# Seven half-size products for two more experts of the second pass, and the last weights' conversion spread over the expert passes

## The chip, the cores and the metric

One core of a Trainium2 chip runs the whole kernel. The metric is the time on the device in microseconds (us), median of the runs; less is better. The engines are TensorE (PE in the profile, PEld its weight loads), VectorE (DVE), ScalarE (ACT), GpSimd (POOL) and SyncE (SP, which only issues DMAs here).

## What is computed

A chain of three stages on 4 x 576 = 2304 tokens of width 512. First a windowed attention with 8 heads. Then a mixture of 8 experts in which every token goes through every expert, weighted by a matrix P that eight rounds of row and column scaling have made:

```
for e in range(8):
    h = np.maximum(x @ w1[e], 0.0)          # 512 -> 1024
    out += P[:, e:e + 1] * (h @ w2[e])      # 1024 -> 512
```

Last, one feed-forward layer with 2048 hidden units, `g(x @ w_in) @ w_out`, where g is a clipped square. `w_in` and `w_out` arrive as 64-bit floats and have to be made 32-bit on the chip. Every 32-bit value is then split into a high and a low part (fp32r), and every product is three matmuls: high x high, high x low, low x high (`product`, L347 to L351).

## The kernel before

Tokens are worked in three passes of 768 (k = 0, 1, 2). A hidden layer is cut in units of 512 hidden columns: an expert is two units (2e and 2e + 1), the feed-forward layer is units 16 to 19. One accumulator `acc` holds the output of the pass.

**First layer of a unit** (`first_layer`, L353): 768 x 512 by 512 x 512 as seven half-size products (a Strassen form; the order is 1, 5, 6, 2, 7, 3, 4), each in two halves q, so 14 steps m = 0 to 13 of six matmuls of 384 columns. At m = 6 to 11 VectorE adds the product to a kept partial sum (L368).

**Second layer** in one of two ways. A unit run (`"u"` in the list of runs) does it plainly: 72 matmuls of 512 columns in 24 steps (`second_layer`). An expert run (`"e"`) takes both units of an expert together and does their second layer as seven half-size products (`seven_second`, L440): 7 products (n = 0 to 6) x 3 token tiles (t = 0, 1, 2) x 12 matmuls of 256 columns = 252. The input of each product is a sum and difference of quarters of the hidden layer (`Seven`, sums on VectorE at L323, high parts on ScalarE at L109, low parts on VectorE at L110), made one step at a time by the tables `FIRST_WORK` and `SECOND_WORK`. After each (n, t) VectorE adds the result into `acc` (L465), in program order with everything else on VectorE. Two 256-column results share one PSUM bank: `halves` (L443) gives t = 0 and t = 2 the two halves of one bank, t = 1 another.

Pass k = 0 runs units singly, since the experts' weights are prepared then. In pass k = 1 the experts named by `WHOLE` (L430) run as two unit runs, the others as expert runs; in pass k = 2 experts 1 to 7 are all expert runs. Expert 0 has its first unit done during the attention and its second one (`u == 1`) as a unit run in each pass.

**The conversion** of `w_in` and `w_out` (`double_steps`, L206) is a generator; each `pull(double)` in the program text puts the next step into the engines' instruction streams at that place. It runs in passes k = 1 and k = 2, and has 14 empty steps, then 352 steps, 88 for each unit: four pieces of `w_in` with seven VectorE operations each (ops 1, 2, 3 and 5 short, ops 4, 6 and 7 long), 28 steps that split that unit's `w_in` (groups of four: a ScalarE copy; a VectorE subtraction; another and a store; a pause), and four pieces of `w_out` with eight steps (the seven operations, then a step with a ScalarE copy, the VectorE subtraction that waits for it, and two stores). It stops at the end of a piece when `at.hold` is set (from expert 6 of pass k = 1 until the first layer of pass k = 2) and then starts again with a load and eight empty steps. What is left at the last expert of pass k = 2 is put out there at once (`drain(double)`).

Every engine works its instructions off in program order, and all DMAs are on SyncE's one queue, also in program order: nothing is reordered at run time.

Of the kernel before, what the change touches and what calls it, by code (L numbers as in the profile page):

```python
# [27 lines left out]
def tile_attention_moe_ffn(ctx: ExitStack, tc, q, k, v, w_gate, w1, w2, w_in, w_out, out):  # L28
# [130 lines left out]
    def prep_w2(u):  # L159
# [3 lines left out]
        for d, (there, here) in enumerate(w2_halves(u)):  # L163
            if d == 0 or u % 2 or u // 2 in WHOLE:
                nc.sync.dma_start(out=there, in_=here)
# [261 lines left out]
                finish(py[t], k * TPP + t)  # L427
            yield "y"

    WHOLE = (1, 2, 3)  # L430

    FIRST_WORK = {1: "h10 h11", 2: "l10", 3: "l11", 4: "s50", 5: "s51 h50", 6: "h51", 7: "l50", 8: "l51",
                  12: "s60 s61", 13: "s70 s71"}
# [436 lines left out]
    def pull(steps, n=1):  # L870
        for _ in range(n):
            next(steps, None)

    with tc.manual_schedule():
# [214 lines left out]
        for k in range(1, NPASS):  # L1089
            runs += [("u", 1, k)]  # L1090
            for e in range(1, E):
                runs += [("u", 2 * e + i, k) for i in range(2)] if k == 1 and e in WHOLE else [("e", e, k)]
        runs += [("u", u, k) for k in range(NPASS) for u in FFN]
# [4 lines left out]
        def input_of(run):  # L1098
            return run[2], units[units_of(run)[0]][0]
# [12 lines left out]
        for n, run in enumerate(runs):  # L1112
            kind, k = input_of(run)[1], run[2]
# [3 lines left out]
            ends = begins(n + 1)  # L1117
# [12 lines left out]
            if run[0] == "u":  # L1130
                u = run[1]
# [49 lines left out]
                for m, s in enumerate(second_layer(k, finish, LAST if u2 is None else SECOND)):  # L1181
                    if fresh and m == 0:
                        if u == 1:
                            load_raw_w2(u2)
                        ahead = prep_w2(u2)
                    if fresh:
                        pull(nxt)
                    if ends and m > 4 and (m % 2 if kind == "ffn" else m % 3 == 0):
                        pull(build)
                    if m > 2 and m % 2:  # L1190
                        at.sink = ("h", 2)
                        pull(sink)
                    if m > 12 or u > 1 and m % 5:
                        pull(double)
                    if m % 3:
                        pull(sums)
# [16 lines left out]
            for m, i in enumerate(first_layer(2 * e, act_kept(0), late)):  # L1213
                if m % 2:
                    pull(nxt)
                if m < 6 or m > 11:
                    pull(double)
                if e == 1 and m >= len(ORDER) * UQ - TPP:
                    t = m - (len(ORDER) * UQ - TPP)
                    nc.scalar.activation(out=acc[:, t, :], in_=acc[:, t, :], func=AF.Copy,  # L1220
                                         scale=prob[:, k * TPP + t, 0:1])
# [14 lines left out]
            for m, i in enumerate(first_layer(2 * e + 1, act_kept(1), late)):  # L1236
                if m % 2:
                    pull(nxt)
                work(ops, FIRST_WORK.get(m, ""))
                if not ends and m < 2:  # L1240
                    pull(double)
            drain(nxt)
            for n_, t in seven_second(e, k, bufs):
                work(ops, SECOND_WORK.get((n_, t), ""))
                if t == TPH - 1:
                    later = n_ + 3
                    if later < len(ORDER):
                        load_op(e, ORDER[later], words(w2_buf[(ring + later) % 3]))
                    elif after[0] == "e":
                        load_op(after[1], ORDER[later - 7], words(w2_buf[(ring + later) % 3]))  # L1250
                if not ends and (n_, t) >= (4, 0):
                    pull(double)
                if ends and (n_, t) in ((1, 2), (2, 2), (3, 2), (4, 1), (4, 2), (5, 0), (5, 1), (5, 2), (6, 0), (6, 1)):
                    pull(build)
# [34 lines left out]
```

## Time and profile before

| | |
|---|---|
| median of 3 runs | 2012.32 us (2011.96 to 2013.23) |
| profiled execution | 2011.22 us, its span 2009.4 us |
| TensorE matmul busy | 1976.8 us, 98% of the span |
| VectorE busy | 1423.2 us, 71% |
| ScalarE busy | 916.4 us, 46% |
| DMA, 16 engines' share | 70.6% |

The span is the time from the first to the last instruction of the profiled execution; the time of that execution is 1.8 us longer, and the median of the runs another 1.1 us. Busy shares are averages over stages with different limits, so the argument goes by stretches: what an expert takes from its first matmul to the next one's, and which wait on TensorE ends when.

### The profile page before, as it was taken

To read this page: it belongs to the slowest core of one execution; us is meant where nothing else is said; L and a number is where in the kernel's file an instruction comes from. 1 tells how busy PE (TensorE), PEld (TensorE's weight loads), DVE (VectorE), ACT (ScalarE), POOL (GpSimd) and SP (SyncE) were. 2 spreads that over 40 slices of the span, in tenths; PEclk is the share of its full clock that TensorE was granted. 3 is DMA by queue.
4 is the path that set the end of the run, shared out by engine and by line. 5 is a ranking of instruction groups with operands and counts; after the bars stand their busy time and mean duration, and the time that the engine had idled before them with its cause. 6 is when DMAs were issued, how large, how long until landed. Compare 5 with 4: busy or idle time off the path is not lost.

```text
span 2009.4 us, 32018 instructions
## 1 busy us (share of the span) xinstructions
PE 1976.8 (98%) x11954; PEld 1839.1 (92%) x11954; DVE 1423.2 (71%) x2575; ACT 916.4 (46%) x2019; POOL 282.3 (14%) x295
## 2 busy tenths in 40 slices
PE   8999999999999999999999999999999999999999
PEld 6887889998998989989999999999999989889898
DVE  6644597888788867776876567776777675766856
ACT  6656445545555443323345435444444444443443
POOL 4212214435445401010000000000000000000000
PEclk9999999999999999999999999999999999999999
DMA  7432567988788887778878877887778856465562
GB/s 173 109 70 85 188 243 269 339 320 306 291 319 324 313 319 293 270 302 315 304 259 289 310 261 283 301 286 274 281 280 287 303 189 222 171 246 204 204 217 88
DMA packets 250044, 507.81 MB, mean 253 GB/s; under 512 B 80032, under 2 KB 155808, under 8 KB 234912
## 3 DMA queue, kind: packets, MB, share of 16 engines
q1 hardware_dynamic: 249888, 505.75, 70.6%
q8 instruction: 95, 1.56, 0.3%
q14 instruction: 61, 0.50, 0.1%
HBM read 355.22 MB, written 150.47 MB: 252 GB/s over the span
## 4 chain that ended last, share of the span: by engine, by line
PE 89%; DVE 6%; ACT 2%; DMA 2%; issue 1%; POOL 0%; SPq 0%; ACTq 0%; POOLq 0%; DVEq 0%
PE py L350 28%; PE pa L350 22%; PE pc L350 10%; PE qy L350 9%; PE pb L350 5%; PE qt L350 5%; PE ph L350 3%; PE s L679 2%; PE qs L350 1%; PE px L721 1%; DVE xf L323 1%; PE pe L705 1%; PE pt L647 1%; PE qx L350 1%; DMA w1o<-w_kept 1%
## 5 line engine op out<-in xcount | busy, mean ns | idle before, releaser
L350 PE MATMUL pa<-xo,w1o 128*128 128x384 f32 x2736 | 516.2, 336 | 4.4 <-ACT kept L365 2.7
L350 PE MATMUL py<-w2o,hh 128*128 128x512 f32 x1680 | 517.6, 389 | 0.0
L350 PEld LDWEIGHTS pa<-xo,w1o 128*128 128x128 f32 x2736 | 478.9, 188 | 9.3 <-ACT kept L365 3.4
L350 PEld LDWEIGHTS py<-w2o,hh 128*128 128x128 f32 x1680 | 314.6, 188 | 62.5
L350 PE MATMUL py<-w2o,hl 128*128 128x512 f32 x840 | 326.8, 389 | 0.0
L136 POOL TENSOR_TENSOR raw<-raw 128x256 f32<-128x256 f32 x152 | 139.7, 948 | 984.6 <-DVE raw L264 501.3
L350 PE MATMUL pc<-xo,w1o 128*128 128x384 f32 x1368 | 257.1, 335 | 1.8 <-DVE w1o L110 1.2
L365 ACT ACTIVATE kept<-pa 128x384 f32<-128x384 f32 x228 | 111.7, 492 | 314.0 <-PE pa L350 312.3
L350 PEld LDWEIGHTS pc<-xo,w1o 128*128 128x128 f32 x1368 | 238.4, 188 | 2.4 <-DVE w1o L110 1.5
L350 PEld LDWEIGHTS py<-w2o,hl 128*128 128x128 f32 x840 | 157.7, 188 | 32.8
L368 DVE TENSOR_TENSOR kept<-pb,kept 128x384 f32<-128x384 f32 x114 | 63.0, 556 | 133.3 <-PE pb L350 133.1
L110 DVE TENSOR_TENSOR w1o<-raw,w1o 128x256 fp32r<-128x256 f32 x210 | 122.8, 631 | 15.7 <-ACT w1o L109 15.5
L350 PE MATMUL pb<-xo,w1o 128*128 128x384 f32 x684 | 129.1, 335 | 0.1
L350 PEld LDWEIGHTS pb<-xo,w1o 128*128 128x128 f32 x684 | 119.0, 188 | 0.4 <-DMA w1o<-w_kept 0.4
L513 ACT ACTIVATE hh<-kept 128x384 fp32r<-128x384 f32 x138 | 72.5, 526 | 100.3 <-DVE kept L368 100.3
L109 ACT ACTIVATE w1o<-raw 128x256 fp32r<-128x256 f32 x210 | 77.3, 414 | 66.7 <-POOL raw L136 66.7
L323 DVE TENSOR_TENSOR xf<-xf 128x768 f32<-128x768 f32 x108 | 99.1, 951 | 0.2
L1064 ACT ACTIVATE xf<-kept 128x384 f32<-128x384 f32 x132 | 68.3, 524 | 63.3 <-DVE kept L368 63.1
L514 DVE SCALAR_TENSOR_TENSOR hl<-kept,hh 128x384 fp32r<-128x384 f32 x138 | 90.7, 661 | 1.9
L539 DVE SCALAR_TENSOR_TENSOR acc<-py,prob,acc 128x512 f32<-128x512 f32 x120 | 84.3, 740 | 9.8 <-PE py L350 9.8
L110 DVE TENSOR_TENSOR third<-xf,third 128x768 fp32r<-128x768 f32 (+1 forms) x82 | 76.7, 943 | 18.4 <-ACT third L109 18.4
L465 DVE SCALAR_TENSOR_TENSOR acc<-qy,prob,acc 128x256 f32<-128x256 f32 x132 | 63.5, 481 | 36.7 <-PE qy L350 33.5
(184 smaller groups left out, 2918.7 us busy)
## 6 DMA issues: line engine op xcount, KB each, us to landing
w1o<-w_kept SPq DMA_DIRECT2D x294, 512.0 KB, 6.1
w2o<-w_kept SPq DMA_DIRECT2D x58, 1024.0 KB, 5.9
w_kept<-w1o SPq DMA_DIRECT2D x105, 512.0 KB, 4.4
w2o<-w_sums SPq DMA_DIRECT2D x32, 1024.0 KB, 5.0
w_kept<-w2o SPq DMA_DIRECT2D x26, 1024.0 KB, 6.4
raw<-in_moe_w_dram SPq DMA_DIRECT2D x15, 1024.0 KB, 9.7
xf<-in_moe_w_dram SPq DMA_DIRECT2D x15, 1024.0 KB, 8.3
w2x<-w_kept SPq DMA_DIRECT2D x15, 1024.0 KB, 4.8
```

The lines of the kernel that those rows point to most:

```text
L109: nc.scalar.activation(out=hi, in_=raw, func=AF.Copy)
L110: return lambda: nc.vector.tensor_tensor(out=lo, in0=raw, in1=hi.bitcast(F32), op=ALU.subtract)
L136: nc.gpsimd.tensor_tensor(out=out[:, q], in0=in0[:, q], in1=in1[:, q], op=op)
L323: nc.vector.tensor_tensor(out=dst, in0=in0, in1=in1, op=ALU.subtract)
L350: nc.tensor.matmul(o, lhsT=a(h), rhs=b(l), start=first and n == 0, stop=last and n == 2, skip_group_check=on)
L365: nc.scalar.activation(out=dst, in_=src, func=AF.Copy)
L368: nc.vector.tensor_tensor(out=dst, in0=src, in1=dst, op=ALU.add)
L465: nc.vector.scalar_tensor_tensor(out=at_, in0=o, scalar=prob[:, k * TPP + x, e:e + 1], in1=at_, op0=ALU.mult, op1=ALU.add)
L513: return [lambda: nc.scalar.activation(out=hi, in_=src, func=AF.Relu), lambda: nc.vector.scalar_tensor_tensor(out=lo, in0=src, scalar=0.0, ...
L514: lambda: nc.vector.scalar_tensor_tensor(out=lo, in0=src, scalar=0.0, in1=hi.bitcast(F32), op0=ALU.max, op1=ALU.subtract)]
L539: nc.vector.scalar_tensor_tensor(out=o, in0=py, scalar=prob[:, t, e:e + 1], in1=o, op0=ALU.mult, op1=ALU.add)
L1064: return [lambda: nc.scalar.activation(out=hid[:, half_, j, f], in_=src, func=AF.Relu)]
```

## The change

Experts 2 and 3 leave `WHOLE`, so they become expert runs in pass k = 1: instead of four unit runs there are two expert runs. The steps of the conversion are pulled at other places:

- the unit run of expert 0 in pass k = 2: in all 24 steps of its second layer instead of 11;
- an expert run's first unit: 8 steps as before, but at odd m and m = 12 instead of m = 0 to 5, 12 and 13;
- its second unit: m = 0, 1, 2 and 9, 10, 11 instead of m = 0, 1;
- its seven products: after t = 1 of every product and after every t of products 4 to 6, and in pass k = 2 after every t of product 3, instead of only after products 4 to 6. An expert run so has 27 steps (k = 1) or 29 (k = 2) instead of 19.

The second half of `w2` is no longer stored for the first units of experts 2 and 3 (L162, by `WHOLE`).

```
-    WHOLE = (1, 2, 3)
+    WHOLE = (1,)
...
-                    if m > 12 or u > 1 and m % 5:
+                    if m > 12 or u > 1 and m % 5 or k > 1:
                         pull(double)
...
             for m, i in enumerate(first_layer(2 * e, act_kept(0), late)):
                 if m % 2:
                     pull(nxt)
-                if m < 6 or m > 11:
+                if m % 2 or m == 12:
                     pull(double)
...
                 work(ops, FIRST_WORK.get(m, ""))
-                if not ends and m < 2:
+                if not ends and (m < 3 or 9 <= m <= 11):
                     pull(double)
...
-                if not ends and (n_, t) >= (4, 0):
+                if not ends and (t == 1 or n_ > 3 or k == 2 and n_ == 3):
                     pull(double)
```

## Rows read from the trace of the kernel before

**Rows 1.** The page: busy time by engine, and engines of the last chain.

```profile
PE 1976.8 (98%) x11954; PEld 1839.1 (92%) x11954; DVE 1423.2 (71%) x2575; ACT 916.4 (46%) x2019; POOL 282.3 (14%) x295
...
PE 89%; DVE 6%; ACT 2%; DMA 2%; issue 1%; POOL 0%; SPq 0%; ACTq 0%; POOLq 0%; DVEq 0%
```

**Rows 2.** Windows, one expert each: stretch and length, then busy us by engine.

```profile
873.01:934.83 61.82, 61.82 (x314) 56.20 (x312) 44.11 (x86) 20.59 (x45) 4.26 (x6) 1.00 0.81 298
934.83:995.91 61.08, 59.89 (x422) 59.27 (x421) 47.37 (x79) 25.16 (x44) 0.00 (x0) 1.00 0.85 315
995.91:1055.20 59.29, 59.29 (x423) 59.29 (x422) 44.22 (x72) 25.47 (x45) 1.79 (x2) 1.00 0.78 269
...
1114.52:1174.45 59.93, 59.57 (x423) 59.37 (x422) 41.05 (x63) 28.20 (x48) 0.00 (x0) 1.00 0.77 278
...
1268.45:1328.08 59.63, 59.55 (x423) 59.35 (x422) 44.73 (x74) 25.38 (x44) 0.00 (x0) 1.00 0.82 291
1328.08:1387.39 59.31, 59.31 (x422) 59.31 (x421) 44.42 (x74) 24.45 (x42) 1.60 (x2) 1.00 0.78 274
```

**Rows 3.** Waits of TensorE, 820 to 1660 us: total us, times, longest.

```profile
PE pa L350 <- DMA w1o<-w_kept: 1.1, 1, 1.1
PE qy L350 <- DVE acc L465: 0.7, 2, 0.4
PE qt L350 <- DVE acc L465: 0.3, 1, 0.3
```

**Rows 4.** Timeline of TensorE, product 4 of the second pass's last expert.

```profile
1160.91 3.02 PE L350 MATMUL qy<-w2o,hh 128*128 128x256 f32 x24
1164.29 1.70 PE L350 MATMUL qy<-w2o,hh 128*128 128x256 f32 x12 [0.36 <-DVE acc L465]
```

**Rows 5.** Timeline of VectorE in the same stretch.

```profile
1162.89 0.95 DVE L323 TENSOR_TENSOR xf<-xf 128x768 f32<-128x768 f32 x1
1163.76 0.47 DVE L465 SCALAR_TENSOR_TENSOR acc<-qy,prob,acc 128x256 f32<-128x256 f32 x1
```

**Rows 6.** Timeline of VectorE, expert 5 of the second pass (begins at 995.91).

```profile
1023.14 0.56 DVE L368 TENSOR_TENSOR kept<-pc,kept 128x384 f32<-128x384 f32 x1 [0.47 <-PE pc L350]
1023.62 3.56 DVE L323 TENSOR_TENSOR xf<-xf 128x768 f32<-128x768 f32 x4
1027.09 0.48 DVE L465 SCALAR_TENSOR_TENSOR acc<-qy,prob,acc 128x256 f32<-128x256 f32 x1
...
1039.59 0.48 DVE L465 SCALAR_TENSOR_TENSOR acc<-qs,prob,acc 128x256 f32<-128x256 f32 x1 [0.94 <-PE qs L350]
...
1045.51 0.68 DVE L253 SCALAR_TENSOR_TENSOR xf<-xf 128x512 int32<-128x512 int32 x1
1046.11 0.47 DVE L465 SCALAR_TENSOR_TENSOR acc<-qy,prob,acc 128x256 f32<-128x256 f32 x1
...
1047.37 0.42 DVE L256 TENSOR_SCALAR xf<-xf 128x512 int32<-128x512 int32 x1
1047.71 0.47 DVE L465 SCALAR_TENSOR_TENSOR acc<-qy,prob,acc 128x256 f32<-128x256 f32 x1
```

**Rows 7.** Timeline of VectorE, expert 2 of the third pass (begins at 1268.45).

```profile
1287.85 0.69 DVE L104 TENSOR_TENSOR raw<-xf,raw 128x512 fp32r<-128x512 f32 x1 [4.31 <-ACT raw L103]
...
1300.15 0.97 DVE L465 SCALAR_TENSOR_TENSOR acc<-qy,prob,acc 128x256 f32<-128x256 f32 x2
```

**Rows 8.** Timeline of VectorE, product 4 of the third pass's expert 1.

```profile
1261.46 0.69 DVE L104 TENSOR_TENSOR raw<-xf,raw 128x512 fp32r<-128x512 f32 x1 [0.30 <-ACT raw L103]
```

**Rows 9.** Groups by form: the conversion's subtractions that split w_in.

```profile
L110 DVE TENSOR_TENSOR raw<-raw,raw 128x256 fp32r<-128x256 f32 x56 | 23.3, 431 | 31.9 <-ACT raw L109 31.8
```

**Rows 10.** Timeline of SyncE where unit runs give way to expert runs.

```profile
935.12 1.08 SPq L276 DMA_DIRECT2D w_kept<-raw  x2
...
938.29 1.44 SPq L170 DMA_DIRECT2D w1o<-w_kept  x2
```

**Rows 11.** Timeline of TensorE in that expert (begins at 934.83).

```profile
950.72 1.48 PE L350 MATMUL pa<-xo,w1o 128*128 128x384 f32 x7 [1.14 <-DMA w1o<-w_kept]
```

More of the change, by code (lines that the diff above doesn't have):

```diff
@@ L428, in second_layer @@
             yield "y"
-    WHOLE = (1, 2, 3)
+    WHOLE = (1,)
     FIRST_WORK = {1: "h10 h11", 2: "l10", 3: "l11", 4: "s50", 5: "s51 h50", 6: "h51", 7: "l50", 8: "l51",
@@ L1192, in tile_attention_moe_ffn @@
                         pull(sink)
-                    if m > 12 or u > 1 and m % 5:
+                    if m > 12 or u > 1 and m % 5 or k > 1:
                         pull(double)
@@ L1215, in tile_attention_moe_ffn @@
                     pull(nxt)
-                if m < 6 or m > 11:
+                if m % 2 or m == 12:
                     pull(double)
@@ L1239, in tile_attention_moe_ffn @@
                 work(ops, FIRST_WORK.get(m, ""))
-                if not ends and m < 2:
+                if not ends and (m < 3 or 9 <= m <= 11):
                     pull(double)
@@ L1250, in tile_attention_moe_ffn @@
                         load_op(after[1], ORDER[later - 7], words(w2_buf[(ring + later) % 3]))
-                if not ends and (n_, t) >= (4, 0):
+                if not ends and (t == 1 or n_ > 3 or k == 2 and n_ == 3):
                     pull(double)
```

## The prediction

> **What bounds the kernel now.** I read the page first, then windows of one expert each, then TensorE's waits, then the timelines around each wait. TensorE is busy 98% of the span and carries 89% of the last chain [rows 1]: a matmul less is time gained, and anything that holds TensorE up is time lost at full price. The windows give the prices [rows 2]. An expert as two unit runs takes 61.82 us (first row), all of it matmul. An undisturbed expert run takes 59.29 to 59.32 us (third and last row). Between them stand disturbed expert runs: 61.08 us for the first one after the unit runs, 59.93 for the last expert of a pass, 59.63 for one that VectorE delayed. From 820 to 1660 us TensorE's waits on these things are one wait for a weight load and three for VectorE's addition into `acc` [rows 3]. Those few show what TensorE depends on, and the change adds VectorE work just there.
>
> **The rule behind the VectorE waits.** Product 4 of the second pass's last expert stands still before its t = 2 and is released by the addition at L465 [rows 4]. VectorE had just finished the addition of t = 0 (1163.76 + 0.47 = 1164.23; TensorE goes on at 1164.29) [rows 4, 5]. t = 0 and t = 2 use the two halves of one bank; so t = 2 of every product begins only when the addition of t = 0 is done, and t = 1's twelve matmuls are all the time that this addition has. The halves don't overlap, and were addresses all that counted, there would be no such wait; the row says there is one. The Trainium skill ("PSUM — Partial Sum Buffer", section "PSUM bank collisions raise a hardware error") tells to guard PSUM by bank and quadrant, not by address. By that rule the wait stands in every product, also where it is too short to show now; by addresses alone the first rival below would hold. The trace sides with the page (0.36 us of idle before t = 2).
>
> How much delay is free is read in two places. **Place A**, product 0: its addition of t = 0 comes straight behind four sums (1023.62 to 1027.18), and these behind the first layer's last addition at 1023.14, with only 0.47 us of idle ahead of that [rows 6]. In expert 2 of the third pass the same addition came at 1300.15, which is 31.70 us from the expert's start instead of 31.18 [rows 6, 7], 0.52 us late, and that expert took 59.63 us instead of 59.31 [rows 2]: 0.32 lost, so 0.2 us of delay is free. **Place B**, product 4: one operation more ahead of its addition moved it by 0.87 us (1162.89 to 1163.76) [rows 5], and that expert took 59.93 us instead of 59.32 [rows 2]: 0.61 lost, 0.26 free.
>
> **The change part by part.** *Two experts as expert runs:* 2 x (61.82 - 59.32) = **5.0 us gained** [rows 2]. The Trainium skill ("TensorE: Matmul & The Clock Gate", section "Back-to-back issue gap") puts a matmul of N columns at N / 2.4 GHz + 2.5 ns; for 144 of 512 against 252 of 256 columns that is an estimate of 31.1 against 27.5 us, 3.5 an expert, and the sum below would be 2 us lower. The rows have 2.5 an expert, and decide.
>
> *The change-over from unit runs to expert runs* moves from expert 4 to expert 2. Now it costs 61.08 - 59.32 = 1.76 us [rows 2]: stores of the conversion hold SyncE until 935.12, the three loads of 1 MB for the first products go out behind them, the weights of the second unit only at 938.29, and TensorE waits 1.14 us for them [rows 10, 11]. With the change the conversion is at step 55 there, the last store of a split `w_in`: one store that waits for a short subtraction, and no load of a next piece behind it. I take **1.5 us gained**, between 0 and 1.76.
>
> *Disturbances that go:* the conversion's steps that delayed experts 1 and 2 of the third pass fall elsewhere. Expert 2 gets 0.32 back [rows 2], expert 1 about 0.5 (its wait on `qt`, 0.3 of idle [rows 3], behind the step in [rows 8]; with the pipeline's restart, in the proportion of 0.61 lost to 0.36 idle in [rows 2, 4]). **0.8 gained.**
>
> *Hidden:* an expert run loads 14 MB where two unit runs load 11 MB, and two stores of 1 MB go in pass k = 0, in which TensorE is the bound. DMA shares of 0.78 to 0.82 in undisturbed expert runs [rows 2], with no wait on a load but the one named [rows 3], cover it; without cover, 3 MB at 298 GB/s is 10 us an expert, the upper end. The 13 more steps in the unit run of pass k = 2 lie in plain products with whole banks: 0, as in the unit runs with 21 steps there now (61.82 us without idle).
>
> *The conversion's steps at new places* decide. A long operation put between others moves what follows by 0.60 us (1045.51 to 1046.11), a short one by 0.34 (1047.37 to 1047.71) [rows 6], a subtraction of the split is short too (0.43) [rows 9]; pauses and ScalarE copies cost VectorE nothing. Which step falls where follows from counting: 55 steps are done when expert 2 of pass k = 1 begins, then 27 an expert, until the hold ends them in expert 6 at step 168; in pass k = 2, 184 are done when expert 1 begins, then 29 an expert. So expert runs begin at step 56, 83, 110, 137, 164 (k = 1, experts 2 to 6) and 185, 214, 243, 272, 301, 330 (k = 2, experts 1 to 6).
>
> Place A gets an expert's 12th to 14th step (m = 9, 10, 11), where no expert run has any now. The first two eat the 0.47 us of idle, the third comes after it: delay = (first two - 0.5, at least 0) + third, loss = delay - 0.2. With L long, S short, 0 none:
> - k = 1: expert 2 SLS 0.6, expert 3 LLS 0.8, expert 4 0SS 0.15, expert 5 LSL 0.8;
> - k = 2: expert 1 LLS 0.8, expert 2 0SS 0.15, expert 4 SLL 0.8, expert 5 00S 0.15, expert 6 SLL 0.8. Expert 3 gets L, L and the step whose subtraction waits for a ScalarE copy. That wait was 0.30 us in one place and 4.31 in another [rows 7, 8]; here the copy stands behind one Relu that waits for VectorE itself, and I take an estimate of 1.2 us, so 0.7 + 1.2 + 0.6 - 0.2 = 2.3.
>
> Together **7.4 us lost**. From below: 0 where VectorE has more air than I see; from above 3 us more, if that one wait is 4.31.
>
> Place B gets, in pass k = 2, all three steps of product 3 (an expert's 18th to 20th), loss = sum - 0.26: expert 1 SLL 1.3, expert 2 S0S 0.4, expert 3 LSL 1.3, expert 4 LSL 1.3, expert 5 SS0 0.4, expert 6 SLS 1.0. **5.7 us lost.** In pass k = 1 it gets one short step an expert, about 0.1 over the free 0.26: 0.3 for the four.
>
> Product 5 waits likewise. Products 4 to 6 have three steps each, as now, but where product 4 has used up its slack the next has 0.2 to 0.4 less. That binds in expert 6 of k = 2, which meets the steps that stopped expert 1 [rows 8], and a little in the two experts 3: **1.5 us lost.** Elsewhere the added steps (after t = 1 of products 0 to 2, odd m of the first unit) find idle ahead of the next addition (0.94 us at product 3 [rows 6]) and cost 0; 0.6 an expert where that is gone.
>
> Sum: -5.0 - 1.5 - 0.8 + 7.4 + 5.7 + 0.3 + 1.5 = +7.6 us. On the profiled 2011.22 that is 2018.8, and the median stands 1.1 above: **2019.9 us**, 0.38% slower.
>
> **The rivals.**
> *VectorE takes it all in:* VectorE is busy 44 of 59 us in an expert run [rows 2], ten more steps bring some 5 us, and on the average there is room. Then only the gains are left, -7.3: 2005.0 us. Against it: the average says nothing of places A and B, and [rows 4, 5, 7] show single operations costing time there.
> *One of the two places binds:* if the additions at product 0 have a us more than I read, or the steps of product 3 find it, the sum is near -7.3 + 7 = 0: about 2012 us. For it: the two thresholds rest on one disturbed expert each. Against: undisturbed expert runs repeat to 0.03 us, so that 0.3 and 0.6 us stand out clearly.
> *ScalarE's copies hold VectorE longer:* VectorE waits in order, and its low parts and sums for the next products stand behind a copy that is itself queued behind high parts. With 4.31 us [rows 7] instead of 1.2 or 0.3 in the two worst experts of pass k = 2, the loss is 5 us more and the change-over gives nothing: 2026.5 us.
> *It doesn't do what it says:* step 352 comes at 23 of expert 6, inside the pulls, so nothing is left over for the last expert; that doesn't change the time.
>
> **How the numbers follow.** My own case 0.68, its range 2014 to 2025 us (losses between 0.6 and 1.25 of the sum of 14.9; at the upper end the change-over gives nothing). One place only 0.14, all taken in 0.12, longer waits 0.06. The range 2010 to 2025.5 holds nearly all of my own case and most of the one-place case, and leaves out 0.2. Differences within 0.2% (4 us, 2008.3 to 2016.3) can't be told from none: faster 0.13 (all taken in, and a little of one place), same 0.2 (one place, and the low end of my own), slower 0.67.
>
> **What would show it.** Right: expert 2 and 3 of pass k = 1 at about 60 us instead of 61.82; in pass k = 2, expert runs 2 and 5 near 59.9, 4 near 61.4, 3 near 63.4; TensorE's waits full of `qy` released by L465, each before t = 2 of product 0 or 4, while the change-over's weight wait is gone or small. Wrong: expert runs of pass k = 2 at 59.3 us with conversions in them, or TensorE's waits on DMA or on low parts (L110), or losses in unit runs.

## The result and the profile after

| | before | changed kernel |
|---|---|---|
| median | 2012.14 us (2008.53 to 2013.23) | 2031.82 us (2026.13 to 2039.83) |
| profiled execution | 2011.22 us | 2039.83 us |
| from the second pass's first matmul to the last one's end | 1290.0 us | 1310.4 us |

The change makes the kernel slower by 1.04% (ratio 1.0104, 95% interval 1.0083 to 1.0125). The sign was forecast. The size was not: 2019.9 us was forecast, and the time lies above the range of 2010 to 2025.5 us.

The profiled execution is 28.6 us longer than the one before, but only 20.4 of them lie where the change is, in the third line of the table. That line is the measure from here on and is called the *stretch*. The other 8.2 us lie in the attention, whose code the change doesn't touch. Windows of that place, first of the changed kernel as profiled, then of a second profile of the same kernel (x15_again, below); the columns are those of [rows 2], the granted clock is third from the end:

```profile
33.00:68.00 35.00, 32.42 (x216) 28.41 (x216) 21.11 (x60) 17.68 (x75) 12.12 (x17) 0.51 0.57 133
```

```profile
33.00:68.00 35.00, 30.96 (x299) 26.68 (x298) 26.86 (x75) 22.47 (x96) 17.20 (x22) 0.87 0.66 153
```

In the first TensorE stands at its lower level (0.5, 1.2 GHz) for nearly all of these 35 us, in the second for about 9 of them. So the 8 us belong to one execution and not to the kernel.

The page of the changed kernel, the answer to [rows 1]:

```profile
PE 1991.6 (98%) x12170; PEld 1859.8 (91%) x12170; DVE 1439.2 (71%) x2605; ACT 937.7 (46%) x2047; POOL 284.3 (14%) x295
...
PE 83%; DVE 12%; DMA 2%; ACT 1%; issue 1%; POOL 0%; DVEq 0%; ACTq 0%; POOLq 0%
```

The busy shares have hardly moved. The chain has: VectorE holds 12% of it instead of 6%. Where, the windows of one expert each show (the answer to [rows 2]): first experts 2 and 3 of the second pass, then experts 1 to 6 of the third. An undisturbed one takes 59.3 us.

```profile
819.43:880.04 60.61, 59.89 (x421) 59.36 (x420) 47.71 (x83) 26.12 (x45) 0.00 (x0) 1.00 0.88 328
880.04:941.14 61.10, 60.15 (x422) 59.41 (x421) 48.01 (x82) 25.03 (x43) 1.61 (x2) 1.00 0.84 293
...
1214.74:1285.66 70.92, 62.93 (x422) 61.91 (x420) 54.15 (x94) 30.17 (x54) 1.77 (x2) 0.95 0.77 277
1285.66:1345.79 60.13, 59.79 (x422) 59.38 (x421) 42.62 (x74) 27.77 (x52) 4.26 (x6) 1.00 0.87 311
1345.79:1410.67 64.88, 61.76 (x422) 60.93 (x421) 48.74 (x84) 26.26 (x45) 0.00 (x0) 0.97 0.81 277
1410.67:1472.07 61.40, 59.83 (x422) 59.42 (x421) 47.42 (x81) 26.00 (x46) 1.79 (x2) 1.00 0.80 284
1472.07:1532.07 60.00, 59.86 (x422) 59.36 (x421) 42.47 (x73) 28.08 (x53) 4.26 (x6) 1.00 0.85 311
1532.07:1594.01 61.94, 60.09 (x422) 59.48 (x421) 46.28 (x79) 26.37 (x45) 0.00 (x0) 1.00 0.82 292
```

The 70.92 us of the third pass's expert 1 stand out most; then come experts 3, 4 and 6 of that pass. What TensorE waited for in the expert passes, 757 to 1660 us (the answer to [rows 3]):

```profile
PE qy L350 <- DVE acc L465: 9.9, 15, 2.0
PE pa L350 <- DMA w1o<-w_kept: 6.7, 2, 6.2
PE qt L350 <- DVE acc L465: 0.9, 2, 0.6
...
```

There are two troubles. Seventeen waits of `qy` and `qt` for the addition at L465 add up to 10.8 us; the prediction has them. It doesn't have the one wait of 6.2 us for a weight load in the third pass. Split by expert run into first layers (29.12 to 29.15 undisturbed) and seven products (30.17), the 20.4 us of the stretch are:

| us | predicted | changed kernel | x15_again |
|---|---|---|---|
| two more expert runs, undisturbed | -5.0 | -5.0 | -5.0 |
| change-over to expert runs, second pass | -1.5 | -1.1 | -1.8 |
| old disturbances gone | -0.8 | -0.9 | -0.9 |
| conversion steps in the seven products | +14.9 | +16.7 | +16.7 |
| change-over, third pass (first layers of expert 1) | 0 | +9.0 | +7.2 |
| first layers of the other expert runs | 0 | +1.6 | +1.6 |
| sum | +7.6 | +20.3 | +17.8 |

The stretch itself grew by 20.4 and 18.0 us.

**The third pass's change-over, followed back.** SyncE's issues around the end of the unit run (start, us, engine and line, transfer), changed kernel:

```profile
1197.73 0.32 SPq L1078 DMA_DIRECT2D z_kept<-xf  x1
1198.15 0.37 SPq L1080 DMA_DIRECT2D acc<-y_kept  x1
...
1199.55 1.21 SPq L225 DMA_DIRECT2D xf<-in_moe_w_out_dram  x1
...
1215.83 1.10 SPq L276 DMA_DIRECT2D w_kept<-raw  x2
...
1221.67 0.42 SPq L187 DMA_DIRECT2D w2x<-w_kept  x1
1222.18 0.86 SPq L187 DMA_DIRECT2D w2o<-w_sums  x2
1223.09 7.06 SPq L170 DMA_DIRECT2D w1o<-w_kept  x6
```

Kernel before:

```profile
1191.09 0.32 SPq L1078 DMA_DIRECT2D z_kept<-xf  x1
1191.51 0.37 SPq L1080 DMA_DIRECT2D acc<-y_kept  x1
...
1193.17 2.38 SPq L225 DMA_DIRECT2D xf<-in_moe_w_out_dram  x2
1195.61 0.68 SPq L187 DMA_DIRECT2D w2x<-w_kept  x1
...
1210.39 2.40 SPq L170 DMA_DIRECT2D w1o<-w_kept  x2
```

The conversion's load (L225) stands behind a store and a load of 1.5 MB each in both kernels. It also leaves at nearly the same point: 1.1 us after the start of the unit run's second layer in the changed kernel (1198.42), 1.4 us after it in the kernel before (1191.78). What the change moves is the first instruction that needs the load. VectorE, changed kernel and then kernel before:

```profile
1211.15 0.43 DVE L246 TENSOR_SCALAR xf<-xf 128x512 int32<-128x512 int32 x1 [11.45 <-DMA xf<-in_moe_w_out_dram]
```

```profile
1202.86 2.05 DVE L529 TENSOR_TENSOR acc<-py,acc 128x512 f32<-128x512 f32 x3 [9.80 <-PE py L350]
...
1207.54 0.42 DVE L246 TENSOR_SCALAR xf<-xf 128x512 int32<-128x512 int32 x1
```

In the kernel before, the conversion's first operation stands behind four of the additions for the unit run's results (L529) and waits for nothing. Pulled 13 steps earlier it stands ahead of all of them: VectorE stands still for 11.45 us until the load has landed, and the additions queue behind it. The conversion's stores, which wait for VectorE, go out at 1215.83; the loads behind them on SyncE wait too. Then three loads of 1 MB for the products leave at once, and the weights of the expert's second unit, which are needed first, follow at 1223.09, 8.35 us after the expert run's start. In the kernel before they followed 2.29 us after it, and the `w2x` load had left long ahead of them. TensorE, changed kernel, and windows of its wait and of the time behind it:

```profile
1236.19 4.18 PE L350 MATMUL pa<-xo,w1o 128*128 128x384 f32 x12 [6.25 <-DMA w1o<-w_kept]
```

```profile
1229.90:1236.20 6.30, 0.06 (x2) 0.04 (x1) 2.31 (x3) 3.08 (x7) 1.37 (x2) 0.90 1.01 416
1235.00:1241.80 6.80, 5.61 (x18) 5.64 (x19) 0.08 (x1) 1.83 (x4) 0.00 (x0) 0.50 1.03 410
```

The DMA engines are full while TensorE waits 6.25 us (share 1.01, 416 GB/s). Its granted clock falls to 0.5 within that wait and stays there for 6.8 us.

### The profile page after: what moved, and what is told of

Its sections match the earlier page's. It is cut to its first block, busy times and chain, and to the rows that moved or that the text cites. A ratio compares the mean times of both kernels' runs of the same rounds, so it can differ in the third digit from the quotient of the medians.

```text
span 2038.1 us, 32545 instructions
## 1 busy us (share of the span) xinstructions
PE 1991.6 (98%) x12170; PEld 1859.8 (91%) x12170; DVE 1439.2 (71%) x2605; ACT 937.7 (46%) x2047; POOL 284.3 (14%) x295
## 4 chain that ended last, share of the span: by engine, by line
PE 83%; DVE 12%; DMA 2%; ACT 1%; issue 1%; POOL 0%; DVEq 0%; ACTq 0%; POOLq 0%
PE py L350 24%; PE pa L350 20%; PE pc L350 10%; PE qy L350 9%; PE pb L350 5%; PE qt L350 5%; PE ph L350 3%; DVE xf L323 3%; PE s L679 2%; DVE kept L368 2%; PE qs L350 1%; DMA w1o<-w_kept 1%; PE px L721 1%; DVE acc L465 1%; PE pt L647 1%
## 5 line engine op out<-in xcount | busy, mean ns | idle before, releaser
L350 PE MATMUL py<-w2o,hh 128*128 128x512 f32 x1488 | 459.2, 390 | 0.0
L350 PEld LDWEIGHTS py<-w2o,hh 128*128 128x128 f32 x1488 | 279.3, 188 | 55.5
L350 PE MATMUL py<-w2o,hl 128*128 128x512 f32 x744 | 289.7, 389 | 0.0
L365 ACT ACTIVATE kept<-pa 128x384 f32<-128x384 f32 x228 | 111.8, 491 | 297.7 <-PE pa L350 296.1
L368 DVE TENSOR_TENSOR kept<-pb,kept 128x384 f32<-128x384 f32 x114 | 63.3, 556 | 163.1 <-PE pb L350 162.1
L350 PEld LDWEIGHTS py<-w2o,hl 128*128 128x128 f32 x744 | 139.8, 188 | 29.1
L1064 ACT ACTIVATE xf<-kept 128x384 f32<-128x384 f32 x156 | 81.3, 524 | 81.2 <-DVE kept L368 81.0
L323 DVE TENSOR_TENSOR xf<-xf 128x768 f32<-128x768 f32 x124 | 113.6, 951 | 0.1
L465 DVE SCALAR_TENSOR_TENSOR acc<-qy,prob,acc 128x256 f32<-128x256 f32 x156 | 74.2, 480 | 38.7 <-PE qy L350 36.6
L513 ACT ACTIVATE hh<-kept 128x384 fp32r<-128x384 f32 x114 | 59.9, 526 | 85.3 <-DVE kept L368 85.3
L109 ACT ACTIVATE third<-xf 128x768 fp32r<-128x768 f32 (+1 forms) x90 | 67.4, 774 | 62.2 <-DVE xf L323 22.3
L350 PE MATMUL qy<-w2x,third 128*128 128x256 f32 x648 | 82.3, 284 | 4.0 <-DVE acc L465 4.0
```

The source lines that it names most:

```text
L109: nc.scalar.activation(out=hi, in_=raw, func=AF.Copy)
L323: nc.vector.tensor_tensor(out=dst, in0=in0, in1=in1, op=ALU.subtract)
L350: nc.tensor.matmul(o, lhsT=a(h), rhs=b(l), start=first and n == 0, stop=last and n == 2, skip_group_check=on)
L365: nc.scalar.activation(out=dst, in_=src, func=AF.Copy)
L368: nc.vector.tensor_tensor(out=dst, in0=src, in1=dst, op=ALU.add)
L465: nc.vector.scalar_tensor_tensor(out=at_, in0=o, scalar=prob[:, k * TPP + x, e:e + 1], in1=at_, op0=ALU.mult, op1=ALU.add)
```

## The experiments

All are edits of the changed kernel unless said otherwise. Ratios are to the kernel before, run on the same chip, with 95% intervals.

### Which part costs: the places of the steps alone

x4_spread_only is the changed kernel with `WHOLE = (1, 2, 3)` again, so the new places without the two expert runs.

> The kernel before with the new places of the conversion alone: experts 2 and 3 of the second pass stay unit runs. Theories 1 and 2: about 14 us slower than before (change-over of the third pass 9.0, VectorE's waits about 5.5, less 0.9 of old ones; fewer expert runs have steps, since the conversion is done in expert 4 of the third pass): about 2026 us. Rival (the loss comes with the two more expert runs and their loads): the time of before, 2012.

Measured: 2023.43 us, 1.0049 [1.0031, 1.0066], stretch 1304.1, 14.1 above before. The window of the third pass's expert 1:

```profile
1208.22:1277.14 68.92, 62.57 (x422) 60.85 (x421) 56.00 (x98) 29.75 (x52) 0.00 (x0) 0.98 0.84 311
```

The new places alone make the kernel slower, and the change-over of the third pass is as long without the two expert runs. VectorE's stop is the same, 11.40 us, but it reaches TensorE by another way: 4.0 us of waiting for a copy by ScalarE (L365) that stands behind a copy of the conversion (L103), and 0.8 us more at the start of the expert's second unit.

With the two expert runs the stretch gets longer still (1308.0 in x15_again), though they are 5 us shorter than four unit runs. Four unit runs took 116 steps of the conversion and two expert runs take 54, so it ends in expert 6 of the third pass and not in expert 4, and other, longer steps fall to products 0 and 3 (5.4 us lost in the third pass's products here, 13.9 in the changed kernel, both with the 0.6 of expert 7).

### The products: VectorE's additions and the shared banks

x2_noA moves the steps of place A (m = 9 to 11 of an expert's second unit) to m = 0 to 2, two each:

```
-                if not ends and (m < 3 or 9 <= m <= 11):
-                    pull(double)
+                if not ends and m < 3:
+                    pull(double, 2)
```

> The changed kernel, but the three steps at m = 9, 10, 11 of an expert's second first layer are put at m = 0, 1, 2 beside the three that stand there, so that every other step keeps its place. Theory 2 (VectorE): the waits of TensorE before t = 2 of product 0 vanish (nine of them, 0.5 to 2.3 us each, together 7.7 us), those of products 4 and 5 stay: about 2024 us. Theory that VectorE is only short of time as a whole: the waits turn up elsewhere and the time stays at 2032. The change-over of the third pass stays as it is (38.7 us).

x3_noB takes, in the third pass, the steps of place B (product 3) to product 6:

```
-                if not ends and (t == 1 or n_ > 3 or k == 2 and n_ == 3):
-                    pull(double)
+                if not ends and (t == 1 and (k == 1 or n_ != 3) or n_ > 3):
+                    pull(double, 2 if k == 2 and n_ == 6 else 1)
```

> The changed kernel, but in the third pass the three steps of product 3 are taken out and three more put after product 6 (two a time there). Theory 2: the waits before t = 2 of product 4 vanish in the third pass (1.31, 0.43, 1.30, 1.31, 0.42, 1.03 us with the matmul's own pace), and that of product 5 in expert 6; the time falls by about 6.5 us to 2025. Those of product 0 stay. Theory that VectorE is only short of time as a whole: no gain.

Measured: x2_noA 2022.72 us, 1.0056 [1.0036, 1.0076], stretch 1301.7; x3_noB 2022.33 us, 1.0048 [1.003, 1.0065], stretch 1300.2. TensorE's waits for L465, first without A, then without B (9.9 us, 15 times with both):

```profile
PE qy L350 <- DVE acc L465: 5.6, 8, 1.0
```

```profile
PE qy L350 <- DVE acc L465: 6.1, 11, 2.0
```

Each place costs: the products lose 9.8 us without A and 16.7 with it; in the third pass 5.2 without B and 13.3 with it (experts 1 to 6). The change-over of the third pass stays in both (first layers of 37.28 and 36.65 us).

x8_banks leaves every step where the change put it and separates the results instead: the accumulators of products 1 and 5 (`i` in the code), which collect six of the seven products, get a third bank each, borrowed from the first layer, so that t = 0 and t = 2 share none.

```
-            if i in (1, 5, 2):
+            if i in (1, 5):
+                z = "y" if i == 1 else "t"
+                chain[i] = [bank(x, 2, f"q{x}{i}")[:, :HD] for x in ("h", z, z)]
+            elif i == 2:
...
-                            of == i and c == 0 and t < 2, c == KC - 1, of != i or t == 2)
+                            of == i and c == 0 and (t < 2 or i != 2), c == KC - 1, of != i or t == 2 and i == 2)
```

> The changed kernel, but the three results of chains 1 and 5 of the seven products lie in three banks (one of the first layer's, which are idle then) instead of two, so that t = 0 and t = 2 share none; nothing else is moved. Theory 2 (t = 2 waits for the addition of t = 0 because of the shared bank): the waits at products 0, 4 and 5 vanish, 16.7 us together, less than 1 us of others comes: from the second pass's first matmul to the last 1294 to 1295 us instead of 1310. Rival (VectorE is short of time as a whole, and the bank is only where it shows first): the waits move to the low parts or to later additions, and less than half is gained. The change-over in the third pass stays at 36.7 to 38.7 us.

Measured: 2015.69 us, 1.0025 [1.0015, 1.0035], stretch 1292.5: 15.5 less than the 1308.0 of x15_again. The clearest reading is expert 3 of the third pass, where the changed kernel lost most in its products. VectorE and TensorE there, changed kernel (the expert begins at 1345.79):

```profile
1375.74 0.69 DVE L104 TENSOR_TENSOR raw<-xf,raw 128x512 fp32r<-128x512 f32 x1 [1.11 <-ACT raw L103]
1376.35 3.56 DVE L323 TENSOR_TENSOR xf<-xf 128x768 f32<-128x768 f32 x4
1379.83 0.87 DVE L465 SCALAR_TENSOR_TENSOR acc<-qy,prob,acc 128x256 f32<-128x256 f32 x2
```

```profile
1375.31 3.03 PE L350 MATMUL qy<-w2o,hl 128*128 128x256 f32 x24
1380.36 1.83 PE L350 MATMUL qy<-w2o,hl 128*128 128x256 f32 x12 [2.01 <-DVE acc L465]
```

The same in x8_banks (the expert begins at 1332.14; the addition is L468 there):

```profile
1366.17 0.48 DVE L468 SCALAR_TENSOR_TENSOR acc<-qh,prob,acc 128x256 f32<-128x256 f32 x1
```

```profile
1364.02 3.04 PE L350 MATMUL qy<-w2o,hl 128*128 128x256 f32 x24
1366.90 1.59 PE L350 MATMUL qh<-w2x,third 128*128 128x256 f32 x12
```

VectorE is exactly as late in both: its first addition comes 34.04 and 34.03 us after the expert's start. But without a shared bank TensorE runs t = 1 and t = 2 (24 matmuls) on while that addition is still outstanding. All waits on the additions are gone in this kernel; what is left of TensorE's waits from 720 to 1640 us is

```profile
PE pa L350 <- DMA w1o<-w_kept: 5.4, 1, 5.4
PE qh L350 <- ACT xf L1067: 0.7, 1, 0.7
PE pa L350 <- ACT xf L1067: 0.2, 1, 0.2
```

The wait of `qh` is the price of the borrowed bank: it comes free only when ScalarE's Relu (L1067) has emptied it. So the loss in the products is the wait on the bank of t = 0, and not VectorE's work as such. The Trainium skill ("PSUM — Partial Sum Buffer", section "PSUM bank collisions raise a hardware error") says that accesses are to be guarded by bank, not by address, and these waits agree. In the changed kernel the shared bank costs 15.5 us.

x10_before_banks makes the same edit in the kernel before.

> The kernel before with the three banks of x8_banks and nothing else. Theory 2: its four waits on the addition at L465 vanish (lost 0.61, 0.61, 0.53 and 0.34 us, rows 2 and 3), and each expert run takes up to 0.1 us more in its products as in x8_banks: 1 to 2 us faster from the second pass's first matmul to the last, 1288 to 1289 us; in the time no difference that can be told.

Measured: 2007.58 us, 0.9982 [0.9961, 1.0002], stretch 1287.8, 2.2 less than before. Every seven products take 30.16 to 30.23 us there. The disturbances that the waits for additions in [rows 3] stand for were all that the shared banks cost before the change.

### The third pass's change-over

Three theories: the 13 added steps in the unit run (x1_unit11), the conversion's late load that stops VectorE (x11_early_load), or the burst of product loads ahead of the weights (x5_hoist, x13_defer).

x1_unit11 puts the unit run's pulls back to 11; the 13 steps are left over for the pass's last experts.

```
-                    if m > 12 or u > 1 and m % 5 or k > 1:
+                    if m > 12 or u > 1 and m % 5:
```

> The changed kernel, but in the unit run of the third pass the conversion has its 11 steps of before instead of 24. Theory 1 (in that unit run the conversion's steps start only when their load has landed, and then hold SyncE, so that the loads for the first expert run go out late): the first expert run's first layers fall from 38.7 us to about 29.7 us, and the wait of 6.58 us for weights in them is gone. Theory 2 (VectorE's additions at products 0, 4 and 5): these waits stay, with other steps behind them (all later steps move by 13), I count about 12 us in the third pass instead of 13.3; 13 steps are left over for the last expert and cost 0 to 1 us. Both together: about 2021 us. Rival (the loss lies in a lower clock in the attention stage, as in the profiled execution): the time stays at 2032.

Measured: 2024.34 us, 1.0068 [1.0046, 1.009], stretch 1302.6. Expert 1's first layers fall from 38.68 to 30.84 us and the weight wait is gone (6.25 us; the 6.58 expected is counted from the start of the matmul ahead), while the products still lose 12.2 us in experts 1 to 6. The steps that are left over cost the last expert 1.7 us.

x5_hoist sends the first product's load ahead of the unit run's second layer.

```
+                if after and after[0] == "e":
+                    ring = 2
+                    load_op(after[1], ORDER[0], words(w2_buf[2]))
                 for m, s in enumerate(second_layer(k, finish, LAST if u2 is None else SECOND)):
...
-                    for x in range(3):
+                    for x in range(1, 3):
```

> The changed kernel, but the load of the first product's weights (1 MB, into a buffer that is free early) is issued ahead of the second layer of the unit run that precedes an expert run, not behind it. Theory 1a (SyncE is held by the conversion's stores and loads, which wait for VectorE, and so 3 MB of product weights go out in one burst ahead of the second unit's weights): 1 MB less in the burst, about 2.5 us, and less time at the lower clock behind the wait: the first expert run's first layers in the third pass fall from 36.7 to 38.7 us to about 33 to 34 us, in the second pass from 29.8 to 29.2. Theory 1b (the weights are late because of the conversion's own loads): no change.

Measured: 2030.55 us, 1.0104 [1.0089, 1.0119], stretch 1307.8; expert 1's first layers 36.69 us where 33 to 34 were expected. The megabyte put ahead of the conversion's load made that later, and VectorE with it:

```profile
1206.53 0.43 DVE L246 TENSOR_SCALAR xf<-xf 128x512 int32<-128x512 int32 x1 [13.63 <-DMA xf<-in_moe_w_out_dram]
```

```profile
PE pa L350 <- ACT acc L1222: 3.1, 1, 3.1
PE pc L350 <- DVE acc L529: 2.4, 1, 2.4
```

The second fence is TensorE's waits from 1205 to 1235 us. The 2.4 us are new: TensorE now waits for the additions themselves. The 3.1 us are what is left of the weight wait, though the view names ScalarE: L1222 scales `acc`, which these matmuls don't read. The trace has the first of the weight loads land 0.14 us before TensorE goes on, as at the 6.25 us wait of the changed kernel. So half of the weight wait went, and a wait for VectorE took its place.

x11_early_load ends the conversion's pause four first-layer steps earlier, so that its load leaves ahead of the 1.5 MB transfers.

```
+                    if u == 1 and k == 2 and m == 10:
+                        at.hold = False
+                        pull(double)
```

> The changed kernel, but in the third pass's unit run the conversion's pause ends at m = 10 of the first layer, with one step, so that its first load is issued ahead of the store of z and the load of acc (1.5 MB each) and not behind them; all later steps come one place earlier. Theory 1c (VectorE stands 11.5 us in the conversion's first operation, because that load lands late, and all that follows on VectorE and on SyncE is late with it): the first operation waits for nothing, the last additions of the unit run and the stores come in time, and the first expert run's first layers fall from 36.7 to 38.7 us to about 30 us; 7 to 8 us faster than the changed kernel. Theory 1a (the burst of 3 MB ahead of the second unit's weights is enough by itself): still 33 us or more.

x13_defer leaves that load late, but sends only the first product's weights at the unit run's end, the other two after the unit weights that are due earlier.

```
-                    for x in range(3):
+                    for x in range(1):
...
+                if runs[n - 1][0] == "u" and m in (9, 11):
+                    load_op(e, ORDER[(m - 7) // 2], words(w2_buf[(ring + (m - 7) // 2) % 3]))
```

> The changed kernel, but behind a unit run two of the three loads of product weights (2 of 3 MB) are issued at m = 9 and 11 of the expert run's first layer, behind the first four loads of the second unit's weights. Theory 1a (burst): the wait for weights (6.58 us) is gone and the first layers of the third pass's first expert run take 31 us or less, in the second pass 29.2. Theory 1c (VectorE late from the conversion's load): the weights come in time, but TensorE stops for VectorE's late additions, as in x5_hoist (2.69 us before the bank of chain 5 in the first layer is free): 31 to 34 us.

Measured: x11_early_load 2023.74 us, 1.0066 [1.0043, 1.0089], stretch 1302.5, expert 1's first layers 30.45 us; x13_defer 2021.92 us, 1.0058 [1.0044, 1.0071], stretch 1302.4, first layers 31.95. In x11_early_load VectorE's first conversion operation starts without a wait, and the weight wait is 1.0 us:

```profile
1190.55 0.42 DVE L246 TENSOR_SCALAR xf<-xf 128x512 int32<-128x512 int32 x1
```

```profile
PE pa L350 <- DMA w1o<-w_kept: 1.0, 1, 1.0
```

Taking away any one of the three (steps, late load, burst) gives back 5 to 6 us of the stretch, so in the changed kernel the cost needs all three in a chain: the added steps put the conversion's first operation ahead of the additions, VectorE stops there for a load that lies behind 3 MB as it did before, SyncE is held by the stores that wait for VectorE, and the burst then stands ahead of the weights. x13_defer leaves VectorE's stop in place (11.33 us) and still loses 2.8 us in expert 1's first layers; x11_early_load loses 1.3.

### Another placement

x6_early puts most steps into the first layers, where VectorE's additions seemed to have air.

```
-                if m % 2 or m == 12:
-                    pull(double)
+                pull(double, 2 if m < 4 else 1)
...
-                if not ends and (m < 3 or 9 <= m <= 11):
+                if not ends and m < 2:
...
-                if not ends and (t == 1 or n_ > 3 or k == 2 and n_ == 3):
+                if not ends and n_ > 3:
```

The unit run has 11 pulls as in x1_unit11.

> The two more expert runs as in the changed kernel, but the conversion's 29 steps of an expert run are put where VectorE has air: 18 in the first unit's first layer (all m, two at m = 0 to 3), 2 in the second unit's, 9 after products 4 to 6 as before; 11 in the third pass's unit run as before. Theories 1 and 2: what is left is the gain of the two expert runs, 5.0 us and some of the change-over: from the second pass's first matmul to the last 1285 us, where before has 1290 and the changed kernel 1310; some 5 us faster than before. A rival (expert runs are costly by themselves, by their loads): slower than before by 2 us or more. What could spoil it: more conversion loads in the first unit, ahead of the second unit's weights, 1 to 3 us at each change-over.

Measured: 2022.11 us, 1.0063 [1.0048, 1.0078], stretch 1302.2, where 1285 was expected. The products came out as expected (30.16 to 30.17 us in most), but the first layers now take up to 35.33 us. TensorE's waits, 720 to 1640 us:

```profile
PE pa L350 <- ACT xf L1064: 5.9, 7, 1.3
PE pa L350 <- DVE kept L368: 4.1, 1, 4.1
PE pa L350 <- ACT kept L365: 4.1, 2, 3.0
```

The waits for the second layer's additions are gone but for those of the two last experts. The new ones lie in the first layers, where the Relu (L1064) stands behind VectorE's partial sums (L368). Part of this isn't VectorE's work but the change-over's trouble again: pulled so closely, the steps come ahead of their data. VectorE stood still for a conversion load ahead of the longest wait (the 4.1 us), and four more times for 1.2 to 2.0 us. So the run doesn't show whether there is air in the first layers:

```profile
824.66 0.43 DVE L246 TENSOR_SCALAR xf<-xf 128x512 int32<-128x512 int32 x1 [7.06 <-DMA xf<-in_moe_w_out_dram]
```

### Putting it together

x9_banks_unit11 joins x8_banks, x5_hoist and x1_unit11; x12_banks_early joins x8_banks and x11_early_load.

> Three banks as in x8_banks, with the early load of x5_hoist and the 11 steps of x1_unit11. Theories 1 and 2 together: nothing is left of the loss but the 13 steps at the last expert (1.7 us in x1_unit11): from the second pass's first matmul to the last about 1285 us, 5 us under before. If the two theories don't cover the loss, it stays above 1290.

> Three banks as in x8_banks and the early load of x11_early_load. Both theories: from the second pass's first matmul to the last 1285 to 1286 us (1292.5 in x8_banks, less 7), 4 us under before; about 2006 us, if before has 2010 beside it.

Measured: x9_banks_unit11 2011.47 us, 1.0012 [1.0001, 1.0023], stretch 1290.5 (about 1285 expected); x12_banks_early 2008.51 us, 0.9987 [0.9971, 1.0002], stretch 1289.7 (1285 to 1286 expected). Both miss, by 4 to 5.5 us: first layers of 30.3 to 31.2 us at the third pass's change-over and in its expert 6, in x12_banks_early also at the second pass's change-over and in expert 3, in x9_banks_unit11 in the last expert, with its left-over steps. At the change-overs of x12_banks_early these are weight waits of 1.4 and 1.3 us. In experts 3 and 6 they are mainly the borrowed bank: `qh` waits for ScalarE to empty it, 2.0 us in x12_banks_early and 1.1 in x9_banks_unit11. In x9_banks_unit11 a wait of 0.9 us for a product's weights in expert 3 comes on top.

x14_all therefore takes x12_banks_early and x13_defer, and moves the steps of place A to the expert's first unit.

```
-                if m % 2 or m == 12:
+                if m < 6 or m % 2 or m == 12:
...
-                if not ends and (m < 3 or 9 <= m <= 11):
+                if not ends and m < 3:
```

> Two more expert runs with all that the runs so far found: three banks, the early load of x11_early_load, two product loads behind the second unit's weights as in x13_defer, and the three steps at m = 9, 10, 11 of the second unit moved to m = 0, 2, 4 of the first. If the gain of the expert runs is there once its two costs are taken off: from the second pass's first matmul to the last 1286 us or less, 2 us under the kernel before with three banks (1287.8) and 4 under before; about 2006 us. If the conversion's steps cost time wherever they are put, as in x6_early: 1288 or more.

Measured: 2002.77 us, 0.9960 [0.9946, 0.9974], stretch 1282.2. This kernel is faster than the changed kernel and than the kernel before. Windows of its third pass's experts 1 and 3, and all of TensorE's waits from 720 to 1640 us:

```profile
1200.67:1260.46 59.79, 59.61 (x421) 59.28 (x420) 49.60 (x86) 29.56 (x54) 1.61 (x2) 1.00 0.81 305
1319.75:1379.47 59.72, 59.58 (x423) 59.26 (x421) 48.84 (x84) 25.97 (x45) 0.00 (x0) 1.00 0.85 304
```

```profile
PE p L1078 <- ACT xf L1079: 1.9, 2, 1.2
PE pa L350 <- ACT xf L1067: 0.2, 1, 0.2
```

Against x10_before_banks, which has the banks and not the change, the stretch is 5.6 us shorter (1287.8 to 1282.2). That is the gain of the two expert runs (5.0) with a little of the change-over: it was there all the time, under some 25 us of losses (16.7 + 7.2 + 1.6 in the table). x14_all also has the loads of the third pass's change-over in another order, but that is not the gain: expert 1 takes 59.79 us there and 59.80 in x10_before_banks. In x14_all experts 2 and 3 of the second pass take 59.69 and 59.29 us instead of two unit runs of 61.82 [rows 2], so 2.1 and 2.5 us gained. The Trainium skill ("TensorE: Matmul & The Clock Gate", section "Back-to-back issue gap") gives N / 2.4 GHz + 2.5 ns for a matmul of N columns by itself. By that formula an estimate for 144 of 512 against 252 of 256 columns is 3.6 us an expert (31.08 less 27.51; the prediction has 3.5). These rows stay at 2.5.

### The changed kernel again

x15_again is the changed kernel, unchanged.

> The changed kernel once more, unchanged. If the 8 us that its first profiled execution lost ahead of the second pass (half the clock for 34 us in the attention stage) belong to the change: the second pass begins some 8 us later than in before again, and the profiled clock is 0.986. If they are an execution's own: the second pass begins at 713 to 719 us as in most runs, and from there to the last matmul it takes 1310 us again.

Measured: 2029.17 us, 1.0086 [1.0063, 1.0109], stretch 1308.0. The second pass begins at 715.05 us (before 715.67, changed kernel as first profiled 723.93), so the 8 us in the attention are not the change's. Seven products and first layers repeat to 0.03 us, but for the two change-overs, where TensorE waits for weight loads: the third pass's first layers 36.84 us instead of 38.68.

## Why the prediction was wrong in size

**Right: the mechanism in the products, and the sign by it.** The rule that t = 2 begins only when the addition of t = 0 is done was the right one: 17 such waits, and x8_banks removes them all by the bank alone. The sizes held by and large: 16.7 us in the products against 14.9 predicted. Loss in the products, predicted and measured: in the third pass expert 1 2.1 and 2.07, expert 2 0.55 and 0.84, expert 4 2.1 and 2.07, expert 5 0.55 and 0.53, expert 6 some 2.6 (the prediction doesn't split its 1.5 for product 5) and 2.62; in the second pass expert 2 0.6 and 0.60, expert 5 0.8 and 0.86.

**Mis-sized terms.** Expert 3 of the third pass lost 5.19 us instead of 4.1. Its wait on ScalarE's copy was estimated well (1.2, measured 1.11); what is over is the clock, for which the prediction has no term: it was at half for 3.4 us after the 2.01 us wait. Where place B is emptied (x3_noB), no such stretch follows, the expert takes 61.95 us instead of 64.88, and what place A alone loses there, 2.26 us, is the 2.3 predicted. Expert 3 of the second pass lost 1.44 instead of about 1.0, expert 4 0.52 instead of 0.15.

**Right, the gains.** The change-over of the second pass gave 1.1 and 1.8 us in the two profiles (1.5 predicted), the old disturbances 0.9 (0.8). The two expert runs give their 5.0 only where nothing disturbs them, as in x14_all. DMA had cover, as the "Hidden" part said: the only waits on loads in the expert runs are at the two change-overs.

**The step that failed** is in that same part: "The 13 more steps in the unit run of pass k = 2 lie in plain products with whole banks: 0, as in the unit runs with 21 steps there now". It cost 9.0 us in the profile and 7.2 in the second one. The argument looked at TensorE's banks alone. It left out that the conversion starts again here with a load behind 3 MB of other transfers, that its first operation, pulled 13 steps earlier, stops VectorE until that load has landed (11.45 us, where it waited for nothing before), and that the stores and loads behind it on SyncE then wait. The unit runs used as the comparison have no such load to begin with: there the conversion is already running. x1_unit11, x11_early_load and x13_defer show this chain by cutting it in three places. Their times, 2021.92 to 2024.34 us, lie inside the forecast range.

**Not foreseen, small:** 1.6 us in the first layers of five other expert runs, with 0.15 to 0.5 us each. Which step does it in each was not followed up, and stays open.

**The rivals.** "VectorE takes it all in" and "one of the two places binds" are out: x2_noA and x3_noB show that both places cost. "ScalarE's copies hold VectorE longer" gave the nearest time, 2026.5, by luck: its reason did not occur (1.11 us, not 4.31). "It doesn't do what it says" is out as well: the conversion's last operation lies in expert 6. None of the four had the change-over of the third pass: terms that the prediction set to 0 had no rival of their own, and the range, made from the terms that were not 0, could not reach the result.

## What to carry to other kernels

A step that is pulled earlier in an in-order stream doesn't get its data earlier: look up when its load leaves the queue and lands, and who stands behind the first instruction that needs it, on its engine and on the queue. Where an engine waits for another to empty an accumulator, ask first whether the wait is for the data or for a bank that two results share; giving each its own bank was worth 15.5 us in the changed kernel, more than any one move of steps or loads, and 2.2 in the kernel before. And a gain that doesn't show may be whole underneath: the 5 us of the two expert runs came out once the waits that came with them were gone.

## What the runs showed of the hardware

A wait doesn't only cost its own length. Within the 6.25 us at the change-over the granted clock fell to 0.5, that is 1.2 GHz, and 5.6 us of matmuls after the wait ran at that level, 2.8 us lost on top: 9.05 of the 9.5 us or so that these first layers take above undisturbed ones (the table's 9.0 is counted from the 29.65 us of the kernel before). The waits of 5.2 to 5.7 us at the same place in x2_noA, x3_noB, x8_banks and x15_again came with 6.8 us at half clock too. Waits of 3.0 to 4.1 us in x4_spread_only, x5_hoist and x6_early came with 3.4 us. With waits of 1.0 and 1.5 us at the change-over, in x11_early_load and x13_defer, the clock stayed at full.

Between these it isn't settled. The wait of 2.01 us in the third pass's expert 3 was followed by 3.4 us at half clock in the changed kernel, x5_hoist, x13_defer and x15_again, and by none in x3_noB. In x11_early_load a wait of 1.75 us was followed by 3.4 us and one of 2.01 us by none. No run was made to tell the reason.

In the first 70 us, in the attention, the time at half clock differed between executions of the same code: 34 us in the first profile of the changed kernel, 38 in that of x1_unit11, 10 in x15_again. The second pass began at 723.93 us in the one and at 715.05 in the other: 8.9 us, as much as the effects studied here, which is why the argument goes by the stretch.
